# A scheduled recurrence and two gated layers on one core: GpSimd gets no tensor work, prices of the scheduler change, eight units keep separate states

## The chip, the cores and the metric

The kernel runs on one core of a Trainium2 chip. TensorE (PE, with its weight loads as PEld), VectorE (DVE), ScalarE (ACT), GpSimd (POOL) and SyncE (SP, which issues all DMAs) each work through a list of instructions of their own, and wait for each other by semaphores. The metric is the device time of one execution in microseconds (us).

## The reference, cut to what matters

```python
for t in range(S):                                   # S = 768, B = 2, H = 8, D = 48
    cur = einsum('bhd,bhe->bhde', u * k[t], v[t])
    y[t] = einsum('bhd,bhde->bhe', r[t], state + cur)
    state = w[t][..., None] * state + einsum('bhd,bhe->bhde', k[t], v[t])
x = y.reshape(B * S, 384)                            # 1536 tokens
xn = x / sqrt(mean(x * x) + 1e-6) * g
x = (silu(xn @ w_gate) * (xn @ w_val)) @ w_out       # 384 -> 1536 -> 384
x = ((x @ w_a) * (x @ w_b)) @ w_out2                 # the same sizes, without silu
```

Everything is float32. The kernel gets float32 products from TensorE in three passes of a rounded high part and a low part of each operand.

## The kernel before, in words

**The recurrence.** Time is cut into 12 units of 128 steps (6 for each of the two batches), and a unit into two halves of 64. `unit()` makes the scores of a half among themselves by levels of 1, 2, 4, 8, 16 and 32 steps: it multiplies the tile X (which holds r, k and the decays of the unit) by decays over growing distances (`upd`, L495 to L503, recorded at L460; T holds the decays, halved in width from level to level), stacks parts of it in RS and KS by small copies (L512 to L519, recorded at L293), multiplies these on TensorE (L524), and puts each level into its place in the score tile AA (fills at L484 and L487, picks at L545). TK holds k and r by tokens for the diagonal (L465 to L470).

Units with a number below `NSR` keep their state in tiles of their own, ST: the state is multiplied by the decay (into TMP, L614), the unit's own products are added (L625), and the output is the sum of two sets of matmuls (L640), one with the scores and one with the state. Such a unit takes one of the two AA tiles for both halves and does fills and picks over 128 partitions. From unit `NSR` on, `stacked()` puts the state under the values V and the weights of the state under the scores in AA, so that one set of matmuls does both (L421); each half has an AA tile, so that fills and picks go over 64 partitions and are twice as many, and four more copies (L389) and the decay (L398) stack the rows.

A unit's output is normalised (L661 to L702; the tiny steps on NS are L671 to L683) and split into high and low part XS.

**The layers.** Tokens are in four blocks of three units. For each layer m, block j and slice f of the 12 slices of the inner width, `front` makes 18 matmuls of 384 columns (L755), the activation (ACT L762), a product (DVE L764) and the split of it (HS, L766 and L767); `back` makes 9 more matmuls (L776). That is a step here: 27 matmuls, 96 steps in all, 48 for each layer. Weights come as 64-bit words in the ring WST of 7 tiles (72 loads); `convert` (L714 to L737) makes two float32 tiles of each by shifts and by an or (L721 to L732), a rounding copy and the subtraction L735. The 36 conversions of layer 0 run beside the first steps, those of layer 1 beside steps 36 to 53.

**The order.** Nothing is written in order by hand. Each task has a rank, its possible engines with a price in ns, and what it reads and writes. `Plan.walk` takes the tasks by rank and by when an engine would be free, puts each on the engine where it would end first, and keeps a clock for each engine; prices with a third entry 1 hold a common port, one at a time. `Plan.issue` does 13 walks with ranks from the walk before, and issues the shortest. In the opening, before the first matmul of a front, TensorE's planned gaps are filled with matmuls on a blank tile (L812, "filler"). So a price changes no work, but the order on all engines. `load` gives the price of a DMA, `vg`, `vgr` and `vgs` those of the two-input operations that may go to VectorE ("V") or GpSimd ("G").

Of the kernel before, what the change touches and what calls it, by code (L numbers as in the profile page):

```python
# [21 lines left out]
UT = 128  # L22
# [6 lines left out]
LEVELS = (2, 4, 8, 16)  # L29
EPS = 1e-6  # L30
OUT = (128, 3, B * S)
NSR = 5


BK, WALKS, FILL0, PACE = 0.15, 13, 900, 1.1
# [4 lines left out]
class Plan:  # L40
# [41 lines left out]
    def walk(self, rank):  # L82
# [35 lines left out]
        for _ in range(n):  # L118
# [34 lines left out]
            if e == "P":  # L153

                fill = fill and self.cols[i] < 2.3
                if fill and start > FILL0:
                    clock[e] = max(clock[e], FILL0)
                    while start - clock[e] >= 110 or credit(clock[e]) < 0:
                        clock[e] += stream(clock[e], 110, 256 / 110)
                        order.append((clock[e], e, None, None))  # L160
                    start = max(start, clock[e])

                if self.cols[i] > 2.3 and not long:
                    start += 87
                long = self.cols[i] > 2.3
                cost = stream(start, cost, self.cols[i])
            if take is not None:
# [72 lines left out]
def rwkv_moe_kernel(  # L240
# [7 lines left out]
    add = plan.add  # L248
# [14 lines left out]
    def v1(n):  # L263
        return (("V", 65 + 1.04 * n),)
# [3 lines left out]
        return (("V", 65 + 1.04 * n, 1),)  # L268

    def vg(n):  # L270
        return (("V", 65 + 1.04 * n, 1), ("G", 240 + 2.08 * n, 1))


    def vgr(n):
        return (("V", 65 + 1.04 * n, 1), ("G", 180 + 1.667 * n, 1))

    def vgs(n):
        return (("V", 65 + 1.04 * n, 1), ("G", 147 + 2.0 * n, 1))

    def act(n):  # L280
        return (("A", 95 + 0.83 * n),)
# [1 line left out]
    def va(n):  # L283
        return (("V", 65 + 0.52 * n, 1), ("A", 95 + 0.83 * n))
# [1 line left out]
    def pe(ns):  # L286
        return (("P", ns),)

    def load(nbytes):
        return (("Q", nbytes / 360.0),)  # L290

    def copy(E, out, in_):
        (E.copy if E is nc.scalar else E.tensor_copy)(out=out, in_=in_)  # L293
# [63 lines left out]
    def dup(fn, *args):  # L357
        return lambda E: fn(E, *args)


    def load_unit(rank, u):
        b, c = divmod(u, NU)
        s, sv = turn(u, X, 2), turn(u, VS, 2)
        add(rank, load(112 * 6144), lambda E: E.dma_start(
            out=X[s], in_=ax[b, c].rearrange("p a b t -> p a (b t)")), w=[("R", s), ("K", s), ("T", s, 1)])
        for par in two:
            rr = slice(64 * par, 64 * par + 64)
            add(rank, load(64 * 1536), dup(lambda E, par, rr: E.dma_start(
                out=VS[sv][par][rr].rearrange("p h d -> p (h d)"), in_=av[u, rr]), par, rr), w=[("v", sv, par)])

    def load_tokens(rank, u):
        b, c = divmod(u, NU)
        k = turn(u, TK, 1)
        add(rank, load(128 * 4608), lambda E: E.dma_start(
            out=TK[k], in_=atk[u]), w=[("tk", k, 0), ("tk", k, 1)])

    def stacked(at, f, u, r_, t64, t64key, yp):
# [7 lines left out]
        for par in two:  # L385
            if first and par == 0:
                continue
            for hf in two:
                add(at + 12 * f, va(256), dup(lambda E, par, hf: copy(  # L389
                    E, AA[par][place[par]].rearrange("p (a f) t -> p a f t", f=2)[:, :, hf],  # L390
                    r_[rows(hf)].rearrange("p (a par t) -> p a par t", par=2, t=64)[:, :, par]), par, hf),
                    r=[("R", s)], w=[("aa", par, 7 + hf)], lock=("aa", par))

        def decay(E):
            for par in two:
                for hf in two:
                    copy(E, PW[place[par], :, hf], t64[rows(hf), :, par])
        add(at + 12 * f, (("V", 280), ("A", 400)), decay, r=[t64key], w=[("pw",)])  # L398
        up = ("up", u)

        def update(E):
# [45 lines left out]
    def unit(rank, drank, u):  # L447
# [60 lines left out]
        def products(at, g):  # L508
# [3 lines left out]
            for hf in two:  # L512
                def stack(E, hf):
                    copy(E, RS[q][rows(hf), :, hf].rearrange("p e (i h) -> p e i h", h=h), rv[rows(hf), :, :, 1])
                add(at, va(256), dup(stack, hf), r=[("R", s)], w=[("rs", q, hf)])
            j = (4 * u + g) % len(KS)
            left = KS[j]
            add(at, va(256), lambda E: copy(E, halves(left.rearrange("p e t -> p (e t)"), h)[:, :, 0], halves(k_, h)[:, :, 0]),
# [13 lines left out]
        def pick(at, key, g, rr, a):  # L532
            h = LEVELS[g]

            def fn(E):
# [7 lines left out]
                d = bank(key)[rr, 0:256].rearrange("p (e i h) -> p e i h", e=8, h=h)  # L543
                m = masks[rr, 1 + g].rearrange("p (x i h) -> p x i h", x=1, h=h)
                E.copy_predicated(o, m.to_broadcast([rr.stop - rr.start, 8, 32 // h, h]), d)  # L545
            where = v1(256) + ((("A", 5.0 * (rr.stop - rr.start)),) if h == 16 else ())
            add(at, where, fn, r=[key, ("aa", a, 0), ("masks",)], w=[("aa", a, 2 + g)], give=key, lock=("aa", a))

        upd(at, 1)
# [17 lines left out]
        for par in two:  # L567
            a = par if ar else sa
            for hf in two:
                def fn(E, par, hf, a):  # L570
                    r1, r2 = slice(64 * par, 64 * par + 32), slice(64 * par + 32 * hf, 64 * par + 32 * hf + 32)
                    copy(E, AA[a][r1].rearrange("p (a f) t -> p a f t", f=2)[:, :, hf, 32:64],
                         bank(lx)[r2, 0:NPAIR * 32].rearrange("p (a t) -> p a t", a=NPAIR))
                add(at + 11 * f, (("A", 160), ("V", 200)), dup(fn, par, hf, a), r=[lx, ("aa", a, 0)],
                    w=[("aa", a, 9 + 2 * par + hf)], give=lx, lock=("aa", a))
        upd(at + 11 * f, 32)
        kp = ("kp", u)
# [67 lines left out]
                r=[("v", sv, par), ("st", i % 3), ("R", s), ("z",)] + [("aa", sa, i_) for i_ in range(13)], w=[yp], take=yp if par == 0 else None)  # L645
        sx, sy = u % len(XT), u % len(Y3)
        xt, y3, ns = XT[sx], Y3[sy], NS[sn]
        add(at + 15 * f, (("A", 150),), lambda E: copy(E, y3, bank(yp)[0:112, 3 * UT:4 * UT]), r=[yp], w=[("y3", sy)], give=yp)
        add(at + 15 * f, (("V", 470), ("A", 380)), lambda E: copy(
            E, xt[0:112], bank(yp)[0:112, 0:3 * UT].rearrange("p (a t) -> p a t", a=3)),  # L650
            r=[yp], w=[("xt", sx, i) for i in range(7)], give=yp)
# [278 lines left out]
```

## Time and profile before

| | |
|---|---|
| median of 3 runs | 642.37 us (641.42 to 643.42) |
| the profiled execution's own time | 642.38 us |
| its span in the trace | 640.6 us |
| granted TensorE clock, mean over the span | 0.964 of full speed |
| PE, DVE, ACT, POOL busy | 597.0, 434.6, 258.6, 141.9 us |
| first matmul of a front | at 81.07 us |

Busy times are sums over the whole span; the stages differ, and the rows below give them stage by stage. A gap in brackets behind a row is the time that the engine stood idle just before, with what released it. Mean times of one instruction include the time in which it waited inside the engine.

### The profile page before, as it was taken

What the parts mean: (1) busy time and instruction counts of PE and PEld (TensorE: products, weight loads), DVE (VectorE), ACT (ScalarE), POOL (GpSimd) and SP (SyncE); (2) the same over time, 40 slices, a digit from 0 to 9 for tenths busy, and PEclk for the clock granted to TensorE, in tenths of its full rate; (3) what the DMA queues carried; (4) which work ended last, traced back from release to release, by engine and by line L of the source; (5) the groups of instructions that cost most, each with busy time, mean ns of one, the idle gap of its engine ahead of it and who ended that gap; (6) DMA issues with size and microseconds to landing.
All of it is one profiled execution on the core that took longest, in us unless ns stands there. A gap on an engine that the chain in (4) does not pass through costs nothing.

```text
span 640.6 us, 12599 instructions
## 1 busy us (share of the span) xinstructions
PE 597.0 (93%) x4977; PEld 555.1 (87%) x4977; DVE 434.6 (68%) x946; ACT 258.6 (40%) x622; POOL 141.9 (22%) x156
## 2 busy tenths in 40 slices
PE   5899998595998998999999998999999999999997
PEld 4677777484987887899899898999999999999997
DVE  4778989999999999988737898972333333233332
ACT  2654568695877553424311556741011011101101
POOL 5236325346354552130000214100000000000000
PEclk8888999598899999999999999999999999999999
DMA  8934265442452221100001446600010001001001
GB/s 215 300 101 126 63 183 181 150 124 100 143 189 86 87 83 53 45 17 2 5 5 33 141 127 218 198 2 0 1 38 1 0 2 38 1 0 38 1 0 38
DMA packets 20363, 50.15 MB, mean 78 GB/s; under 512 B 3600, under 2 KB 8208, under 8 KB 20304
## 3 DMA queue, kind: packets, MB, share of 16 engines
q1 hardware_dynamic: 20304, 49.35, 25.4%
q8 instruction: 39, 0.64, 0.4%
q14 instruction: 20, 0.16, 0.1%
HBM read 46.38 MB, written 2.36 MB: 76 GB/s over the span
## 4 chain that ended last, share of the span: by engine, by line
PE 59%; DVE 19%; DMA 8%; ACT 6%; issue 5%; SPq 1%; POOL 1%; DVEq 0%; ACTq 0%; POOLq 0%
PE ps L755 34%; PE ps L776 17%; DMA WST<-wt 6%; DVE X L460 2%; DVE WST L730 2%; PE ps L640 2%; PE ps L812 2%; DVE AA L545 2%; DVE WST L732 2%; PE ps L524 2%; DMA X<-ax 1%; DVE W L735 1%; ACT WST L726 1%; DVE HS L767 1%; SPq L654 1%
## 5 line engine op out<-in xcount | busy, mean ns | idle before, releaser
L755 PE MATMUL ps<-XS,W 128*128 128x384 f32 x1728 | 344.5, 343 | 21.5 <-DVE W L735 6.8
L755 PEld LDWEIGHTS ps<-XS,W 128*128 128x128 f32 x1728 | 303.9, 191 | 30.2 <-ACT H L762 10.4
L776 PE MATMUL ps<-HS,W 128*128 128x384 f32 x864 | 176.2, 336 | 3.6 <-DVE HS L767 3.6
L776 PEld LDWEIGHTS ps<-HS,W 128*128 128x128 f32 x864 | 151.4, 188 | 4.6 <-DVE HS L767 3.9
L762 ACT ACTIVATE H<-ps 128x384 f32<-128x384 f32 x96 | 47.1, 490 | 223.7 <-PE ps L755 203.2
L764 DVE TENSOR_TENSOR H<-ps,H 128x384 f32<-128x384 f32 x96 | 53.3, 556 | 83.9 <-ACT H L762 81.5
L293 DVE CAST HS<-H 128x384 fp32r<-128x384 f32 x66 | 25.7, 389 | 71.6 <-PE ps L776 71.5
L767 DVE TENSOR_TENSOR HS<-H,HS 128x384 fp32r<-128x384 f32 x90 | 53.2, 591 | 3.2 <-ACT HS L293 1.0
L721 ACT ACTIVATE WST<-WST 128x384 f32<-128x384 f32 x72 | 40.4, 562 | 26.5 <-DMA WST<-wt 25.8
L735 POOL TENSOR_TENSOR W<-WST,W 128x384 fp32r<-128x384 f32 x20 | 28.7, 1436 | 93.6 <-ACT W L293 48.1
L524 PEld LDWEIGHTS ps<-RS,KS 112*64 112x64 f32 x768 | 28.7, 149 | 16.0 <-issue 6.7
L730 DVE SCALAR_TENSOR_TENSOR WST<-WST 128x384 uint32<-128x384 uint32 x72 | 41.3, 585 | 0.2
L732 DVE SCALAR_TENSOR_TENSOR WST<-WST 128x384 uint32<-128x384 uint32 x72 | 41.0, 581 | 0.2
L293 ACT COPY RS<-X 48x256 f32<-48x256 f32 x74 | 30.2, 408 | 26.4 <-DVE X L460 17.4
L524 PE MATMUL ps<-RS,KS 112*64 112x64 f32 x768 | 35.3, 240 | 5.5 <-ACT RS L293 5.4
L460 DVE TENSOR_TENSOR X<-X,T 112x512 f32<-112x512 f32 x47 | 35.3, 751 | 5.2 <-ACT KS L293 2.5
L812 PE MATMUL ps<-H 128*128 128x256 bf16 x257 | 37.8, 299 | 1.1 <-DVE H L811 1.1
L293 ACT CAST W<-WST 128x384 fp32r<-128x384 f32 x59 | 31.6, 546 | 16.3 <-DVE WST L732 13.3
L545 DVE COPY_PREDICATED AA<-masks,ps 64x256 f32<-64x256 int32 (+1 forms) x64 | 33.4, 522 | 5.3 <-PE ps L524 3.5
L726 ACT ACTIVATE WST<-WST 128x384 uint32<-128x384 uint32 x62 | 34.1, 552 | 0.0
L735 DVE TENSOR_TENSOR W<-WST,W 128x384 fp32r<-128x384 f32 x52 | 31.8, 618 | 1.4 <-ACT W L293 1.1
L812 PEld LDWEIGHTS <-H 128*128 128x128 bf16 x257 | 25.7, 107 | 6.8 <-DVE H L811 1.1
(87 smaller groups left out, 496.5 us busy)
## 6 DMA issues: line engine op xcount, KB each, us to landing
WST<-wt SPq DMA_DIRECT2D x72, 384.0 KB, 3.7
X<-ax SPq DMA_DIRECT2D x12, 672.0 KB, 5.2
TK<-atk SPq DMA_DIRECT2D x12, 576.0 KB, 4.0
V<-av SPq DMA_DIRECT2D x24, 96.0 KB, 4.0
out<-XT SPq DMA_DIRECT2D x12, 192.0 KB, 1.9
XT<-Y SPq DMA_DIRECT2D x72, 8.0 KB, 2.6
u<-au SPq DMA_DIRECT2D x1, 192.0 KB, 4.0
masks<-cms SPq DMA_DIRECT2D x1, 80.0 KB, 10.3
```

The source lines that it names most:

```text
L293: (E.copy if E is nc.scalar else E.tensor_copy)(out=out, in_=in_)
L460: E.tensor_tensor(out=o, in0=a, in1=b_, op=ALU.mult)
L524: E.matmul(out=bank(key)[o:o + 64, 64 * (e // 2):64 * (e // 2) + 64], lhsT=left[:, e], rhs=RS[q][:, e].rearrange("p f t -> p (f t)"), star ...
L730: add(rank, vp(384), lambda E: E.scalar_tensor_tensor(out=x, in0=e, scalar=3, in1=x, op0=ALU.logical_shift_left, op1=ALU.bitwise_or), r=[t ...
L732: add(rank, vp(384), lambda E: E.scalar_tensor_tensor(out=x, in0=e, scalar=0x80000000, in1=x, op0=ALU.bitwise_and, op1=ALU.bitwise_or), r= ...
L735: add(rank, vg(384), lambda E: E.tensor_tensor(out=lo, in0=x.bitcast(F32), in1=hi.bitcast(F32), op=ALU.subtract), r=[tx, ("w", f, i, 0)], ...
L755: E.matmul(out=t, lhsT=W[f][:, a, 3 * which + kk], rhs=XS[j][:, b_, kk], start=(i == 0 and kk == 0), stop=(i == 2 and kk == 2),)
L762: add(n - boost, (("A", 375),), lambda E: E.activation(out=h, in_=gv[0][:, 0:BLK], func=AF.Silu if m == 0 else AF.Copy), r=[("gv", 0)], w= ...
L764: add(n - boost, v1(BLK), lambda E: E.tensor_tensor(out=h, in0=gv[1][:, 0:BLK], in1=h, op=ALU.mult), r=[("gv", 1)], w=[("h", qh)], wait=89)
L767: add(n - boost, vg(BLK), lambda E: E.tensor_tensor(out=hs[:, 1], in0=h, in1=hs[:, 0].bitcast(F32), op=ALU.subtract), r=[("h", qh), ("hs", ...
L776: E.matmul(out=acc[d], lhsT=W[f][:, a, 6 + d], rhs=hs[:, b_], start=(f == 0 and i == 0), stop=(f == NF - 1 and i == 2),)
L812: plan.filler = lambda E: E.matmul(out=gv[1][:, 0:256], lhsT=blank[:, 0:128], rhs=blank, start=True, stop=True, skip_group_check=True)
```

## The change

The prices of `vg`, `vgr` and `vgs` lose their GpSimd entry, so that GpSimd keeps only the memsets of the opening. `NSR` goes from 5 to 8: units 5, 6 and 7 keep separate states as units 0 to 4 do. The other edits are prices: a switch of TensorE between the long matmuls of the layers and the small ones now costs 90 ns both ways (before: 87 ns, one way), loads are dearer where X and TK are read, and small copies, picks and the decay are dearer.

```diff
-NSR = 5
+NSR = 8
...
-                if self.cols[i] > 2.3 and not long:
-                    start += 87
+                if (self.cols[i] > 2.3) != long:
+                    start += 90
...
     def vg(n):
-        return (("V", 65 + 1.04 * n, 1), ("G", 240 + 2.08 * n, 1))
+        return (("V", 65 + 1.04 * n, 1),)
     def vgr(n):
-        return (("V", 65 + 1.04 * n, 1), ("G", 180 + 1.667 * n, 1))
+        return (("V", 65 + 1.04 * n, 1),)
     def vgs(n):
-        return (("V", 65 + 1.04 * n, 1), ("G", 147 + 2.0 * n, 1))
+        return (("V", 65 + 1.04 * n, 1),)
...
-    def load(nbytes):
-        return (("Q", nbytes / 360.0),)
+    def load(nbytes, rate=380.0):
+        return (("Q", nbytes / rate),)
...
-        add(rank, load(112 * 6144), lambda E: E.dma_start(
+        add(rank, load(112 * 6144, 200.0), lambda E: E.dma_start(
...
-        add(rank, load(128 * 4608), lambda E: E.dma_start(
+        add(rank, load(128 * 4608, 250.0), lambda E: E.dma_start(
...
-        add(at + 12 * f, (("V", 280), ("A", 400)), decay, r=[t64key], w=[("pw",)])
+        add(at + 12 * f, (("V", 400, 1), ("A", 760)), decay, r=[t64key], w=[("pw",)])
...
-                add(at, va(256), dup(stack, hf), r=[("R", s)], w=[("rs", q, hf)])
+                add(at, (("V", 260, 1), ("A", 400)), dup(stack, hf), r=[("R", s)], w=[("rs", q, hf)])
...
-            where = v1(256) + ((("A", 5.0 * (rr.stop - rr.start)),) if h == 16 else ())
+            where = (("V", 440 if rr.stop - rr.start == 64 else 335),) + ((("A", 8.3 * (rr.stop - rr.start)),) if h == 16 else ())
...
-                add(at + 11 * f, (("A", 160), ("V", 200)), dup(fn, par, hf, a), r=[lx, ("aa", a, 0)],
+                add(at + 11 * f, (("A", 265), ("V", 260)), dup(fn, par, hf, a), r=[lx, ("aa", a, 0)],
```

The order of the built program shows three places. The first is VectorE at the start of unit 0 (X_85 is unit 0's X, X_86 unit 1's; the rows are those behind the reduction into DG_94). Before, these stand there:

```order
L460 TENSOR_TENSOR T_88<-X_85 112x256
L293 COPY RS_75<-X_85 48x8x32
L484 TENSOR_TENSOR AA_79<-maskd,DG_94 128x512
L460 TENSOR_TENSOR X_85<-X_85,T_88 112x2x128x2
L487 COPY_PREDICATED AA_79<-masks,DG_94 128x256
L293 COPY KS_78<-X_85 112x64x4
```

With the change the same place on VectorE reads:

```order
L460 TENSOR_TENSOR X_85<-X_85 112x2x256
L460 TENSOR_TENSOR T_88<-X_85 112x256
L293 COPY KS_77<-X_85 112x128x2
L293 COPY RS_75<-X_85 48x8x32
L484 TENSOR_TENSOR AA_79<-maskd,DG_94 128x512
L460 TENSOR_TENSOR X_85<-X_85,T_88 112x2x128x2
L460 TENSOR_TENSOR T_89<-T_88 112x128
L293 COPY KS_78<-X_85 112x64x4
L293 COPY RS_76<-X_85 48x8x32
```

The first product on X_85 and the halvings of T, which were GpSimd's, now stand between VectorE's own, and two more small copies are VectorE's. Over the program 138 operations on tensors move from GpSimd to VectorE, and VectorE's list grows from 946 to 1068 instructions.

The second place is TensorE at the first matmul of a front (XS_105 and W_118 are block 0 and slice 0; ps_64 and ps_65 are the two halves of a front). Before:

```order
L524 MATMUL ps_62<-RS_76,KS_78 64x64 x8
L755 MATMUL ps_64<-XS_105,W_118 128x384 x6
L755 MATMUL ps_65<-XS_105,W_118 128x384 x3
L755 MATMUL ps_64<-XS_105,W_118 128x384 x3
L755 MATMUL ps_65<-XS_105,W_118 128x384 x3
L640 MATMUL ps_63<-AA_80,V_81 64x64
```

With the change:

```order
L812 MATMUL ps_65<-H_107 128x256
L524 MATMUL ps_62<-RS_76,KS_78 64x64 x8
L755 MATMUL ps_64<-XS_105,W_118 128x384 x3
L581 MATMUL ps_63<-ident,X_86 128x112 x4
L755 MATMUL ps_64<-XS_105,W_118 128x384 x3
L599 MATMUL ps_62<-V_83,KT 64x48
```

The transposes (L581) and products (L599) of unit 4 now stand between the matmuls of the first front, where before unit 3's output (L640) stood behind most of it. Ahead of the first front the list holds 302 fillers instead of 257.

The third place is VectorE's picks of unit 5, which is the first one that changes its kind. Before, each level is picked twice over 64 partitions, with AA_79 and AA_80 for the two halves:

```order
L460 TENSOR_TENSOR X_137<-X_137,T_90 112x2x32x8
L545 COPY_PREDICATED AA_80<-masks,ps_63 64x128x2
L621 TENSOR_TENSOR V_139<-TMP,ps_61 48x4x48 x2
L545 COPY_PREDICATED AA_79<-masks,ps_62 64x64x4
L545 COPY_PREDICATED AA_80<-masks,ps_62 64x64x4
```

With the change a level is picked once over 128 partitions, into AA_80 alone:

```order
L545 COPY_PREDICATED AA_80<-masks,ps_62 128x64x4
L767 TENSOR_TENSOR HS_109<-H_107,HS_109 128x384
L732 SCALAR_TENSOR_TENSOR WST_112<-WST_112 128x384
L735 TENSOR_TENSOR W_125<-WST_111,W_125 128x384
L487 COPY_PREDICATED AA_80<-masks,DG_95 128x256
L730 SCALAR_TENSOR_TENSOR WST_113<-WST_113 128x384
L545 COPY_PREDICATED AA_80<-masks,ps_63 128x128x2
L545 COPY_PREDICATED AA_80<-masks,ps_61 128x32x8
```

In VectorE's list as a whole the picks over 64 partitions go from 46 to 28, those over 128 from 18 to 25; on TensorE L640 goes from 152 matmuls to 240 and L599 from 80 to 120, L421 from 112 to 64 and L405 from 96 to 56.

## Rows read from the trace of the kernel before

**Rows 1.** The page, busy time, share and instructions of each engine.

```profile
PE 597.0 (93%) x4977; PEld 555.1 (87%) x4977; DVE 434.6 (68%) x946; ACT 258.6 (40%) x622; POOL 141.9 (22%) x156
```

**Rows 2.** Windows: stretch, length, busy time of each engine, granted clock, DMA share, GB/s.

```profile
0.00:81.00 81.00, 71.14 (x1005) 55.53 (x1005) 59.95 (x144) 36.27 (x94) 35.19 (x57) 0.87 0.58 159
81.00:118.00 37.00, 28.66 (x332) 23.47 (x327) 33.93 (x65) 27.80 (x65) 14.34 (x9) 0.94 0.67 193
118.00:174.00 56.00, 46.25 (x369) 40.58 (x370) 52.27 (x119) 41.23 (x99) 25.73 (x21) 0.83 0.36 123
174.00:279.00 105.00, 97.71 (x1013) 88.70 (x1012) 100.90 (x216) 56.65 (x152) 43.59 (x50) 1.00 0.28 86
...
426.00:640.00 214.00, 210.72 (x1216) 210.40 (x1214) 67.89 (x139) 28.29 (x58) 0.00 (x0) 1.00 0.03 12
```

**Rows 3.** Groups by form on POOL, whole span: busy us, mean ns, idle before.

```profile
L735 POOL TENSOR_TENSOR W<-WST,W 128x384 fp32r<-128x384 f32 x20 | 28.7, 1436 | 93.6 <-ACT W L293 48.1 <-PE ps L755 21.5 <-DVE W L293 16.5
...
L484 POOL TENSOR_TENSOR AA<-maskd,DG 64x512 f32<-64x512 f32 x2 | 13.8, 6902 | 8.7 <-DVE DG L468 8.7
```

**Rows 4.** Groups by form on DVE, whole span.

```profile
L767 DVE TENSOR_TENSOR HS<-H,HS 128x384 fp32r<-128x384 f32 x90 | 53.2, 591 | 3.2 <-ACT HS L293 1.0
...
L730 DVE SCALAR_TENSOR_TENSOR WST<-WST 128x384 uint32<-128x384 uint32 x72 | 41.3, 585 | 0.2
L732 DVE SCALAR_TENSOR_TENSOR WST<-WST 128x384 uint32<-128x384 uint32 x72 | 41.0, 581 | 0.2
...
L460 DVE TENSOR_TENSOR X<-X,T 112x512 f32<-112x512 f32 x47 | 35.3, 751 | 5.2 <-ACT KS L293 2.5 <-PE ps L561 2.3
...
L735 DVE TENSOR_TENSOR W<-WST,W 128x384 fp32r<-128x384 f32 x52 | 31.8, 618 | 1.4 <-ACT W L293 1.1 <-PE ps L755 0.2
...
L545 DVE COPY_PREDICATED AA<-masks,ps 64x256 f32<-64x256 int32 x46 | 24.2, 527 | 2.2 <-ACT AA L293 0.9 <-PE ps L524 0.5
...
L484 DVE TENSOR_TENSOR AA<-maskd,DG 64x512 f32<-64x512 f32 x12 | 11.1, 925 | 1.3 <-PE ps L421 1.2
...
L683 DVE SCALAR_TENSOR_TENSOR NS<-NS 128x1 f32<-128x1 f32 x36 | 9.8, 272 | 0.4
```

**Rows 5.** The same view from 300 to 346 us, where POOL is nearly idle.

```profile
L460 DVE TENSOR_TENSOR X<-X,T 112x512 f32<-112x512 f32 x3 | 2.1, 695 | 1.4 <-PE ps L561 1.4
...
L683 DVE SCALAR_TENSOR_TENSOR NS<-NS 128x1 f32<-128x1 f32 x9 | 1.4, 158 | 0.2
...
L484 DVE TENSOR_TENSOR AA<-maskd,DG 64x512 f32<-64x512 f32 x1 | 0.7, 689 | 0.6 <-PE ps L421 0.6
```

**Rows 6.** The same view from 440 to 620 us, where POOL does nothing.

```profile
L767 DVE TENSOR_TENSOR HS<-H,HS 128x384 fp32r<-128x384 f32 x39 | 21.8, 559 | 1.4
```

**Rows 7.** Timeline, 106 to 118 us: start, length, instruction [idle before].

```profile
107.30 6.38 POOL L484 TENSOR_TENSOR AA<-maskd,DG 64x512 f32<-64x512 f32 x1 [2.49 <-DVE DG L468]
...
110.35 1.02 DVE L730 SCALAR_TENSOR_TENSOR WST<-WST 128x384 uint32<-128x384 uint32 x2
...
112.81 1.28 DVE L735 TENSOR_TENSOR W<-WST,W 128x384 fp32r<-128x384 f32 x1
...
116.31 1.33 PE L755 MATMUL ps<-XS,W 128*128 128x384 f32 x3 [6.61 <-DVE W L735]
```

**Rows 8.** Waits of DVE, 0 to 92 us: total, times, longest.

```profile
DVE TK L460 <- DMA TK<-atk: 7.2, 2, 3.6
...
DVE AA L545 <- PE ps L524: 3.0, 3, 1.2
...
DVE RS L293 <- POOL X L460: 1.4, 1, 1.4
```

**Rows 9.** The page's groups: fillers on PE.

```profile
L812 PE MATMUL ps<-H 128*128 128x256 bf16 x257 | 37.8, 299 | 1.1 <-DVE H L811 1.1
```

**Rows 10.** Timeline of PE, 81 to 82 us: the first front.

```profile
81.07 1.33 PE L755 MATMUL ps<-XS,W 128*128 128x384 f32 x6
```

**Rows 11.** The chain that ended last, 30 to 60 us: start, length, what.

```profile
41.50 2.05 PE ps L640 x24
```

More of the change, by code (lines that the diff above doesn't have):

```diff
@@ L388, in stacked @@
             for hf in two:
-                add(at + 12 * f, va(256), dup(lambda E, par, hf: copy(
+                add(at + 12 * f, (("V", 260, 1), ("A", 410)), dup(lambda E, par, hf: copy(
                     E, AA[par][place[par]].rearrange("p (a f) t -> p a f t", f=2)[:, :, hf],
@@ L647, in unit @@
         xt, y3, ns = XT[sx], Y3[sy], NS[sn]
-        add(at + 15 * f, (("A", 150),), lambda E: copy(E, y3, bank(yp)[0:112, 3 * UT:4 * UT]), r=[yp], w=[("y3", sy)], give=yp)
+        add(at + 15 * f, (("A", 210),), lambda E: copy(E, y3, bank(yp)[0:112, 3 * UT:4 * UT]), r=[yp], w=[("y3", sy)], give=yp)
         add(at + 15 * f, (("V", 470), ("A", 380)), lambda E: copy(
```

## Prediction

> **What bounds the kernel now.** I read the page's busy line first [rows 1]. PE is busy for 93% of the span and looks like the bound throughout; the windows say otherwise [rows 2]. From 426 us on PE is busy 210.72 of 214 us and GpSimd does nothing: the end is PE's queue, and whatever is late at 426 us is late at the end. Between 81 and 279 us it is VectorE that is full: 33.93 of 37, 52.27 of 56 and 100.90 of 105 us, together 187.1 of 198 us (94%), while PE has 8.3, 9.8 and 7.3 us idle, together 25.4 us. Up to 81 us, where the first front starts [rows 10], VectorE has 21.05 us idle and PE's list is padded with fillers. So three things decide: how much VectorE has to do until about 279 us, how much of its idle time before 81 us goes, and whether PE gets more work than the 25.4 us cover. The groups by form and the quiet windows [rows 3 to 6] give the prices, the timeline and the waits [rows 7, 8] the places.
>
> **GpSimd's work moves to VectorE.** 138 operations move, with 141.9 us of GpSimd's busy time less its memsets. Two like operations of VectorE of 0.55 us each took 1.02 us back to back [rows 7], so the second costs 0.47 us, and I take 0.09 us off each duration. A two-input operation on 128x384 takes 559 ns where GpSimd is idle [rows 6], so 0.47; 47 of those that move have that size (20 of L735, 6 of L767, 2 of XS, 14 of TK, 5 of V): 47 x 0.47 = 22.1 us. X products are 17, at 695 - 90 ns [rows 5]: 10.3 us. The AA fills are 3 at 0.60: 1.8 us. The narrower ones have no row of their own; between a step on one column (158 - 90 = 70 ns, [rows 5]) and 470 ns for 384 columns I take a straight line, an estimate: 8 of 256 columns at 0.34, 10 of 128 at 0.20, 8 of 64 at 0.14, 24 below that at 0.09, 6 of TMP at 0.27, 15 of SQ at 0.20, together 12.6 us (if all cost the 70 ns of the smallest, 5; at 470 ns each, 33). Sum: 46.8 us.
>
> **What VectorE gets back.** The same forms are faster where GpSimd is quiet. Against rows 4: L767 591 against 559 ns, times 90: 2.9 us. L735 618 against 559, times 52: 3.1. L730 and L732 585 and 581 against the same 559 (their size is the same), times 72 each: 1.9 and 1.6. X products 751 against 695, times 47: 2.6. L484 925 against 689, times 12: 2.8. L683, on a single column, 272 against 158, times 36: 4.1. That is 19.0 us on 223.5 us of busy time, 8.5%. The other forms have 211 us; I take the same share on two thirds of them, since products that read PSUM may not meet GpSimd at all: 12 us. Back come 31 us (19 if the rest gives nothing, 37 if all of it does).
>
> In the trace this is a contention that both sides pay: GpSimd's fill of 64x512 took 6.38 us, and L735 beside its end 1.28 instead of 0.56 us [rows 7]; GpSimd's mean for that fill was 6902 ns, for L735 1436 ns [rows 3]. The Trainium skill (SBUF — State Buffer, section "SBUF: two separate sides") says that the port pair shared by GpSimd and VectorE is an exclusive lock, held for the whole instruction, and the loser fully blocks. The trace agrees that GpSimd blocks (6.38 us for the fill); it shows VectorE's operations running on beside it, so it doesn't show VectorE locked out for GpSimd's busy time. By that rule every us in which GpSimd holds the pair comes back to VectorE's two-input operations, and more would return than the means show.
>
> **Three units change their kind.** By the counts of the order, VectorE and GpSimd together: picks fall by 9 net, at about 0.52 us [rows 4]: -4.7 us. Fills L484 and L487 fall by 3 each at 0.69 [rows 5]: -4.1. Products and sums on V fall by 8 at 0.55, those on TMP and ST rise by 8 at about 0.35 (half the columns): -1.6. Copies: 13 fewer of AA and PW, 16 more of RS, KS and W on VectorE, all about 0.3: +0.9. Sum -9.5 us (the copies at nothing or twice as many: -10 to -8).
>
> So VectorE has 46.8 - 31 - 9.5 = +6 us to do (0 to +18 by the bounds of the contention), nearly all before 279 us, where nothing covers it.
>
> On PE L640 rises by 88 matmuls at 2.05 / 24 = 0.085 us [rows 11], and 40 more of L599 stand against 48 of L421 and 40 of L405 that go. These have no row here; at the same 0.085 they give -4.1 us, so the sum is +3.4, and +7.5 if they were free. It lies between 118 and 240 us, where PE has idle time; I cost it at nothing. If the cover is gone, 4 us.
>
> **Idle time of VectorE in the opening.** Up to 92 us it waits 1.4 us for GpSimd's X product, and twice 3.6 us for TK [rows 8]; the first of the two is the load at the start and stays, the second is unit 2's, and in the new order more of unit 0's and 1's work (GpSimd's before) stands ahead of it, so that the load has landed. Of the 3.0 us in which it waits for L524, half can be filled by what is moved. Together -6.5 us (0, if the longer serial list opens gaps of its own, to -12).
>
> The first front will not start earlier for this: VectorE has more to do before it, and PE has 45 more fillers at 37.8 / 257 = 0.147 us [rows 9], 6.6 us, beside more of unit 4. I expect it at 86 to 92 us instead of 81.07. The work that is done before is missing later: unit 4's transposes stand in the first front now.
>
> **The stretch from 81 us on.** PE lost 6.61 us in one gap, waiting for a conversion's L735 [rows 7], while GpSimd sat on the fill that the plan had priced at 180 + 1.667 x 512 = 1034 ns. The order was made for a chip on which that fill takes 1 us. With no operation priced so wrongly, VectorE's list should wait less at such places; I take two thirds of this gap, -4.5 us (0 to -6.6). The prices of copies, loads and switches move things I can't name one by one; I cost them at nothing, with 3 us to either side: the conversions' stretch behind 350 us has the same work as before.
>
> **Sum.** +6 - 6.5 - 4.5 + 0 = -5 us against the profiled execution's 642.38 us (span 640.6 us and 1.8 us around it), which is the median of the runs to within 0.01 us: 637 us. Range of this case alone: 631 to 640.
>
> **The rivals.** *VectorE gains less than it takes over.* If the contention returns only the 19 us that rows 4 to 6 show, VectorE has 46.8 - 19 - 9.5 = +18 us to do; the 6.5 us of idle time go with it and the gap at 116 us does not shrink, since VectorE is later, not earlier: +11.5, or 654 us; halfway to the forecast's contention 648 us. It decides from the point where the return falls below 46.8 - 9.5 - 6.5 - 4.5 = 26 us. For it speaks that VectorE is 94% busy from 81 to 279 us and now the only engine for this work; against it, that L683's loss of 114 ns on a single column shows a contention the big forms hide.
>
> *The lock gives back more.* GpSimd is busy 83.7 us between 81 and 279 us [rows 2]. If VectorE's operations stand still for more of this than their mean times show, and 45 us instead of 31 come back, VectorE falls by 8 us instead of rising by 6. PE can then regain at most its idle 25.4 us, less 4 us of new work; with half of that, 10.5 us, and 1.5 more for the opening, 630 us. (This is the direction in which the lock of the Trainium skill's page on SBUF would take it.) Against it: beside the fill of 6.38 us VectorE's rows run on at 0.55 us.
>
> *Nothing is left over.* The 6 us more and the idle time less cancel: 641 to 644 us. For it speaks that both terms are small against their bounds.
>
> **How the numbers follow.** Forecast (637) 0.34, the lock (630) 0.13, nothing left 0.19, VectorE the loser (648) 0.34. Within 0.3% (1.9 us) is about what a measurement of this kernel can't tell from no change. A small part of the forecast (down to 640.4) counts as faster, so faster 0.47, same 0.19, slower 0.34. The range 628 to 650 leaves out the far ends of the first rival and of the lock.
>
> **What would show it.** The first L755 at 86 to 92 us; VectorE's busy time between 81 and 279 us still 93% or more of the stretch; L683 near 160 ns and L484 near 690 ns all over the span; L767 near 559. The stretch behind 426 us unchanged in its rate. The forecast is wrong if VectorE's busy time up to the last unit has grown by more than 10 us, if PE's gaps behind L735 are as large as before, or if PE shows less than 10 us idle between 81 and 279 us and is itself the bound there.

## The result, and the profile after

| | before | after |
|---|---|---|
| median on the same chip | 642.37 us (641.42 to 643.42) | 624.03 us (620.85 to 624.5) |
| span of the profile shown | 640.6 us | 623.5 us |
| ratio | | 0.97 [0.9645, 0.9755] |

The forecast was 637 us with a range of 628 to 650; the change brought 18.3 us, over three times the 5 us forecast. One slow execution of each kernel (660.92 us before; 722.55 us after, at a granted clock of 0.746) is left out here, as such ones are of every ratio below, and since the recorded profile is of the latter, every row of after here is from a second set of runs of the same program (e1 below), whose profiled execution took 625.35 us.

The page's busy line after:

```profile
PE 599.8 (96%) x5102; PEld 557.8 (89%) x5102; DVE 432.3 (69%) x1068; ACT 251.3 (40%) x607; POOL 4.8 (1%) x18
```

Beside [rows 1]: GpSimd has gone from 141.9 us to its memsets, VectorE does 122 instructions more (1068 against 946), and yet it is busy 2.3 us less. The windows of after (columns as in [rows 2]):

```profile
0.00:81.00 81.00, 76.57 (x1115) 59.39 (x1116) 63.52 (x183) 36.59 (x98) 4.77 (x18) 0.94 0.61 171
81.00:118.00 37.00, 31.03 (x279) 25.88 (x277) 35.33 (x92) 28.31 (x67) 0.00 (x0) 0.97 0.56 175
118.00:174.00 56.00, 52.26 (x532) 46.46 (x532) 55.45 (x141) 46.04 (x114) 0.00 (x0) 0.93 0.47 146
174.00:279.00 105.00, 100.43 (x1074) 91.88 (x1071) 101.72 (x255) 51.29 (x139) 0.00 (x0) 1.00 0.24 71
...
426.00:620.00 194.00, 193.67 (x1118) 193.35 (x1116) 61.49 (x125) 25.46 (x53) 0.00 (x0) 1.00 0.03 10
```

Between 81 and 279 us VectorE is fuller still (192.5 of 198 us, before 187.1), the granted clock is higher (0.93 against 0.83 from 118 to 174 us), and behind 426 us PE is full as before. Fixed times mix the stages of two kernels, though. So both are cut where the same work of the layers is done: at the first matmul of step 24 (the 649th long matmul: 24 x 27 = 648). In before:

```profile
0.00:278.80 278.80, 243.56 (x2709) 208.08 (x2710) 246.85 (x539) 161.95 (x408) 118.84 (x135) 0.92 0.44 129
...
278.80:640.60 361.80, 353.43 (x2270) 346.98 (x2268) 187.71 (x407) 96.62 (x214) 23.01 (x21) 1.00 0.12 39
```

and after:

```profile
0.00:263.30 263.30, 245.96 (x2834) 210.83 (x2835) 241.00 (x633) 154.87 (x394) 4.77 (x18) 0.96 0.46 136
...
263.30:623.50 360.20, 353.84 (x2270) 346.92 (x2268) 191.33 (x436) 96.44 (x213) 0.00 (x0) 1.00 0.13 40
```

The time up to step 24 is VectorE's busy time and its idle time: 246.9 + 31.9 before, 241.0 + 22.3 after. So of the 17.1 us between the spans 5.9 are less work of VectorE, 9.6 less idle time of it, and 1.6 lie behind step 24. This is a sum and not yet a cause; the experiments ask what the parts of it do. The forms of VectorE after (shape and count; busy us, mean ns; idle before):

```profile
L767 DVE TENSOR_TENSOR HS<-H,HS 128x384 fp32r<-128x384 f32 x96 | 53.4, 556 | 1.9
...
L460 DVE TENSOR_TENSOR X<-X,T 112x512 f32<-112x512 f32 x60 | 41.3, 689 | 1.8 <-PE ps L561 1.4 <-ACT RS L293 0.2
L732 DVE SCALAR_TENSOR_TENSOR WST<-WST 128x384 uint32<-128x384 uint32 x72 | 39.2, 552 | 0.2
L735 DVE TENSOR_TENSOR W<-WST,W 128x384 fp32r<-128x384 f32 x72 | 39.2, 551 | 1.0 <-ACT W L293 0.5 <-PE ps L755 0.2
...
L683 DVE SCALAR_TENSOR_TENSOR NS<-NS 128x1 f32<-128x1 f32 x36 | 5.6, 156 | 0.3
...
L484 DVE TENSOR_TENSOR AA<-maskd,DG 64x512 f32<-64x512 f32 x8 | 5.5, 684 | 0.2
```

Against [rows 4] each is back at its price in the quiet stretch [rows 5, 6]: from 591 to 556 ns for L767, and from 272 to 156 ns for the single column of L683. Waits of DVE, 0 to 92 us (total, times, longest), and two places of PE's timeline:

```profile
DVE RS L293 <- PE ps L524: 4.5, 2, 4.3
DVE AA L545 <- PE ps L524: 3.7, 2, 2.6
DVE TK L460 <- DMA TK<-atk: 3.4, 1, 3.4
```

```profile
85.21 0.76 PE L755 MATMUL ps<-XS,W 128*128 128x384 f32 x3 [1.11 <-DVE W L293]
...
115.40 0.79 PE L755 MATMUL ps<-XS,W 128*128 128x384 f32 x3 [1.55 <-DVE W L735]
```

Beside [rows 8] the wait for POOL and the second wait for TK are gone, but those for L524 grew from 3.0 to 8.2 us. The first front starts at 85.21 us instead of 81.07 [rows 10], and the gap behind L735 near 115 us is 1.55 us instead of 6.61 [rows 7].

### The profile page after: what moved, and what is told of

The parts are those of the page before. It is cut to its first block, busy times and chain, and to the rows that moved or that the text cites. A ratio compares the mean times of both kernels' runs of the same rounds, so it can differ in the third digit from the quotient of the medians.

```text
span 720.8 us, 12726 instructions
## 1 busy us (share of the span) xinstructions
PE 708.9 (98%) x5102; PEld 624.5 (87%) x5102; DVE 437.2 (61%) x1068; ACT 253.2 (35%) x607; POOL 4.8 (1%) x18
## 4 chain that ended last, share of the span: by engine, by line
PE 94%; DVE 4%; DMA 1%; issue 0%; SPq 0%; ACT 0%; ACTq 0%; DVEq 0%
PE ps L755 51%; PE ps L776 25%; PE ps L812 5%; PE ps L524 4%; PE ps L640 4%; PE ps L599 1%; DMA X<-ax 1%; PE ps L581 1%; PE ps L421 1%; PE ps L561 1%; DVE X L460 1%; PE ps L405 1%; DVE WST L732 1%; PE ps L685 0%; DVE W L735 0%
## 5 line engine op out<-in xcount | busy, mean ns | idle before, releaser
L755 PE MATMUL ps<-XS,W 128*128 128x384 f32 x1728 | 405.3, 390 | 2.3 <-DVE W L735 1.5
L755 PEld LDWEIGHTS ps<-XS,W 128*128 128x128 f32 x1728 | 337.3, 201 | 31.5 <-DVE W L735 1.6
L776 PE MATMUL ps<-HS,W 128*128 128x384 f32 x864 | 211.7, 388 | 1.6 <-DVE HS L767 1.6
L776 PEld LDWEIGHTS ps<-HS,W 128*128 128x128 f32 x864 | 169.5, 201 | 16.2 <-DVE HS L767 2.0
L767 DVE TENSOR_TENSOR HS<-H,HS 128x384 fp32r<-128x384 f32 x96 | 53.5, 557 | 6.3 <-ACT HS L293 4.0
L812 PE MATMUL ps<-H 128*128 128x256 bf16 x302 | 50.1, 323 | 1.1 <-DVE H L811 1.1
L460 DVE TENSOR_TENSOR X<-X,T 112x512 f32<-112x512 f32 x60 | 41.3, 688 | 4.9 <-PE ps L561 4.6
L293 ACT COPY RS<-X 48x256 f32<-48x256 f32 x69 | 28.2, 408 | 39.7 <-DVE X L460 24.8
L524 PEld LDWEIGHTS ps<-RS,KS 112*64 112x64 f32 x768 | 30.6, 159 | 12.7 <-issue 9.4
L812 PEld LDWEIGHTS <-H 128*128 128x128 bf16 x302 | 31.7, 112 | 10.8 <-DVE H L811 1.1
L735 DVE TENSOR_TENSOR W<-WST,W 128x384 fp32r<-128x384 f32 x72 | 39.3, 552 | 1.1 <-ACT W L293 0.5
L730 DVE SCALAR_TENSOR_TENSOR WST<-WST 128x384 uint32<-128x384 uint32 x72 | 39.2, 553 | 0.0
L524 PE MATMUL ps<-RS,KS 112*64 112x64 f32 x768 | 36.9, 251 | 1.6 <-DVE NS L680 1.1
L545 DVE COPY_PREDICATED AA<-masks,ps 64x256 f32<-64x256 int32 (+1 forms) x53 | 27.5, 519 | 7.7 <-PE ps L524 6.3
L293 ACT COPY AA<-ps 32x128 f32<-32x128 f32 (+1 forms) x84 | 21.6, 257 | 16.1 <-PE ps L524 5.7
```

Of the source, the lines that this page charges most:

```text
L460: E.tensor_tensor(out=o, in0=a, in1=b_, op=ALU.mult)
L524: E.matmul(out=bank(key)[o:o + 64, 64 * (e // 2):64 * (e // 2) + 64], lhsT=left[:, e], rhs=RS[q][:, e].rearrange("p f t -> p (f t)"), star ...
L735: add(rank, vg(384), lambda E: E.tensor_tensor(out=lo, in0=x.bitcast(F32), in1=hi.bitcast(F32), op=ALU.subtract), r=[tx, ("w", f, i, 0)], ...
L755: E.matmul(out=t, lhsT=W[f][:, a, 3 * which + kk], rhs=XS[j][:, b_, kk], start=(i == 0 and kk == 0), stop=(i == 2 and kk == 2),)
L767: add(n - boost, vg(BLK), lambda E: E.tensor_tensor(out=hs[:, 1], in0=h, in1=hs[:, 0].bitcast(F32), op=ALU.subtract), r=[("h", qh), ("hs", ...
L776: E.matmul(out=acc[d], lhsT=W[f][:, a, 6 + d], rhs=hs[:, b_], start=(f == 0 and i == 0), stop=(f == NF - 1 and i == 2),)
```

## The experiments

All sixteen kernels are read by the same sum: time to step 24 (VectorE's busy + idle), then the time behind it. The second part is 355 to 363 us in all of them. There is one profile of each. Times are medians; ratios are against runs of the kernel before on the same chip, with 95% intervals, and aren't always the quotients of the medians beside them.

### The change run again (e1), and GpSimd's work on VectorE in the old order (e2)

> The changed kernel as it is, for an undisturbed profile. Every theory expects the time already seen, 621 to 625 us. Theory 1 (VectorE: it loses nothing to GpSimd any more) expects VectorE's busy time between 81 and 279 us at or below the 187.1 us of before, L683 near 160 ns, L484 near 690 ns, and the layers' steps ahead of the old kernel's from 118 us on. Theory 2 (clock: TensorE is busier and keeps its full clock) expects the granted clock of the stretch 81 to 174 us, 0.94 and 0.83 before, at 0.97 or more, and VectorE no less loaded than before.

621.11 us (620.25 to 625.35), ratio 0.98 [0.9734, 0.9865]; the kernel before took 636.2 us on that chip, and its 19 runs lay between 629.65 and 642.44. Neither theory had all its signs: VectorE's busy time between 81 and 279 us rose to 192.5 us (Theory 1 had it at or below 187.1, while L683 at 156 ns and L484 at 684 came as it said), and the granted clock was 0.97 and 0.93 from 81 to 118 and from 118 to 174 us (Theory 2 had 0.97 or more in both).

In e2 the walk still counts on GpSimd, but its operations are issued on VectorE at the places where GpSimd had them:

```diff
-                self.tasks[i][2](self.engines[e])
+                self.tasks[i][2](self.engines["V" if e == "G" and len(self.cost[i]) > 1 else e])
```

> The kernel before with its old plan, but every operation that the plan gave to GpSimd is issued on VectorE at the same place of the order (138 operations; the memsets stay). Work and order of everything else are the same. Theory 1 (contention): what comes back is as much as what is added, so 632 to 643 us although the plan thinks two engines work; L683 near 160 ns. Theory 2 (the order, made with true prices, is what matters): VectorE's list is longer in an order that doesn't know it, 643 to 655 us.

641.72 us (640.25 to 645.49), ratio 1.012 [1.0054, 1.0186]. Windows to step 24 and behind it:

```profile
0.00:279.90 279.90, 239.60 (x2709) 202.90 (x2710) 258.82 (x654) 162.21 (x407) 4.76 (x18) 0.95 0.43 128
...
279.90:640.40 360.50, 353.57 (x2269) 346.93 (x2268) 188.60 (x431) 96.81 (x216) 0.00 (x0) 1.00 0.12 40
```

Taken over in all: 258.82 + 188.60 = 447.4 us, 12.8 more than before. The prediction had 46.8 - 31 = 15.8. So taking the work off GpSimd and changing nothing else costs VectorE 13 us, and the kernel wins nothing by it: by the ratio it is 1.2% slower. The profile is 1.1 us later at step 24, since VectorE has 12.0 us more to do there and 10.9 us less idle time (31.9 became 21.1), in the old order.

### The parts alone and in pairs (e3 to e8)

Each is a part of the change, made in the kernel before. G (e3, with N in e8, with P in e6) takes the GpSimd entry from `vg`, `vgr` and `vgs`:

```diff
     def vgr(n):
-        return (("V", 65 + 1.04 * n, 1), ("G", 180 + 1.667 * n, 1))
+        return (("V", 65 + 1.04 * n, 1),)
```

N (e5, with P in e7) keeps eight states apart:

```diff
-NSR = 5
+NSR = 8
```

P (e4) is all other prices of the change, as in:

```diff
-                if self.cols[i] > 2.3 and not long:
-                    start += 87
+                if (self.cols[i] > 2.3) != long:
+                    start += 90
...
-        add(at + 12 * f, (("V", 280), ("A", 400)), decay, r=[t64key], w=[("pw",)])
+        add(at + 12 * f, (("V", 400, 1), ("A", 760)), decay, r=[t64key], w=[("pw",)])
```

> The kernel before with only the GpSimd entries of the three price functions taken away; prices and five separate states as before. Theory 1 expects most of the gain here: 625 to 632 us. Theory 2 expects half or less, 632 to 642 us, since the prices of copies and loads are still wrong.

> The kernel before with only the new prices (switches, loads, small copies, picks); GpSimd keeps its entries and five units keep separate states. Theory 1 expects little: 637 to 645 us. Theory 2 expects at least half of the gain, 626 to 634 us, and a granted clock of 0.98.

> The kernel before with only NSR 8 instead of 5: units 5 to 7 keep separate states; GpSimd and the old prices stay. So far: prices alone gave -6.5 us, no GpSimd alone -1.2, the whole change -15. Theory A (the parts add up, and the states are worth the rest): 627 to 630 us. Theory B (the parts need each other: only a plan with all true prices uses the freed VectorE time): 634 to 642 us, no change.

> The changed kernel with NSR back at 5: no GpSimd work and new prices, five separate states. Theory A (the states are worth 7 us): 626 to 630 us. Theory B: 620 to 624 us, as fast as the whole change.

> The changed kernel with GpSimd's entries back: new prices, eight separate states. Theory A (GpSimd alone is worth 1 us): 621 to 625 us. Theory B: 628 to 633 us, as slow as the prices alone.

> The changed kernel with the old prices of switches, loads, copies and picks: no GpSimd work, eight separate states. Theory A: 626 to 630 us (the prices' 6.5 us are missing). Theory B: 632 to 638 us, since without the prices the rest is worth nothing, as in the run without GpSimd.

e3 and e4 came as Theory 2 had it, e6 as Theory A, e7 as Theory B; e5 fell between its two theories, and e8 came out faster than both.

| parts | run | median | ratio | to step 24: DVE busy + idle | DVE busy in all |
|---|---|---|---|---|---|
| none | before | 636.2, 637.82 on these chips | 1 | 246.9 + 31.9 | 434.6 |
| G | e3 | 634.99 | 0.9972 [0.9932, 1.0012] | 247.2 + 25.1 | 442.5 |
| P | e4 | 629.75 | 0.9948 [0.9925, 0.9972] | 248.1 + 24.6 | 430.3 |
| N | e5 | 630.93 | 0.9894 [0.9815, 0.9974] | 235.9 + 38.7 | 425.0 |
| G, P | e6 | 628.46 | 0.9865 [0.9811, 0.9919] | 247.9 + 18.5 | 444.5 |
| P, N | e7 | 632.83 | 0.9925 [0.9895, 0.9955] | 243.2 + 30.1 | 430.5 |
| G, N | e8 | 625.22 | 0.9816 [0.9755, 0.9877] | 237.1 + 24.2 | 427.3 |
| G, P, N | e1 | 621.11 | 0.98 [0.9734, 0.9865] | 241.0 + 22.3 | 432.3 |

The rows to step 24 of e4, e6 and e7, in this order:

```profile
0.00:272.70 272.70, 244.50 (x2768) 209.87 (x2769) 248.06 (x531) 161.24 (x404) 140.02 (x153) 0.95 0.43 132
0.00:266.40 266.40, 241.95 (x2735) 205.73 (x2735) 247.87 (x637) 160.81 (x408) 4.77 (x18) 0.96 0.44 135
0.00:273.30 273.30, 247.21 (x2851) 212.34 (x2852) 243.17 (x540) 151.86 (x379) 103.78 (x134) 0.96 0.44 132
```

Those of e5 and of e8, the widest pair (eight states with GpSimd, and without):

```profile
0.00:274.60 274.60, 246.65 (x2771) 211.61 (x2772) 235.95 (x530) 153.30 (x380) 109.68 (x129) 0.93 0.42 131
```

```profile
0.00:261.30 261.30, 239.42 (x2753) 203.80 (x2754) 237.11 (x620) 161.07 (x410) 4.76 (x18) 0.97 0.44 137
```

GpSimd's 109.68 us are gone, VectorE issues 90 instructions more and is busy 1.2 us more; its idle time falls by 14.5. In all four pairs the removal of G lowers the idle time (31.9 to 25.1, 24.6 to 18.5, 38.7 to 24.2, 30.1 to 22.3), and the busy time to step 24 moves by -2.2 to +1.2 us. The parts don't seem to add: by the ratios G alone brings 0.3%, which can't be told from zero, 0.8% beside N (e5 to e8) or beside P (e4 to e6), and 1.25%, 8 us, beside both (e7 to e1). N alone brings 1.1%, but beside P, with GpSimd at work, it makes the kernel 3 us slower (e4 to e7).

Not much can be built on one such step. Each row is one order, and the last experiments show orders of one kernel that lie 19 us apart. The profile of before is of an execution 6 us above its median on this chip, so most of the first pair's 6.8 us of idle time isn't in the medians (636.2 and 634.99 us). And e6 is 6.3 us ahead of e4 at step 24, but 5.8 us longer behind it (355.1 and 360.9 us). What all four pairs agree on is the sign of the idle time.

And e3 against e2 shows what the walk does with the knowledge that GpSimd is out:

```profile
0.00:272.30 272.30, 241.06 (x2684) 204.32 (x2685) 247.24 (x625) 167.86 (x427) 4.76 (x18) 0.94 0.45 132
...
272.30:635.00 362.70, 353.97 (x2270) 346.73 (x2268) 195.22 (x446) 95.84 (x213) 0.00 (x0) 1.00 0.13 39
```

Up to step 24 VectorE has 247.24 us instead of e2's 258.82. ScalarE has 4.7 us more in all (263.7 against 259.0) and VectorE 5.0 us less (copies of AA and RS for the most part); VectorE's work behind step 24, where PE is the limit and VectorE has room, grew from 188.6 to 195.2 us.

### Is VectorE's work the price? GpSimd busy beside it (e9), its work doubled (e10)

In e9 the order of all engines is that of after, and GpSimd gets 216 products of 128x128 that nobody needs, on weights that a conversion has just made (they add work, and leave none out):

```diff
+            if m == 0:
+                for k in range(6):
+                    nc.gpsimd.tensor_tensor(
+                        out=scratch, in0=hi[:, k % 3].bitcast(F32), in1=lo[:, k % 3].bitcast(F32), op=ALU.mult)
```

> The changed kernel with its order unchanged on VectorE, TensorE, ScalarE and SyncE; beside each of layer 0's 36 conversions GpSimd multiplies six pieces of 128x128 of the converted weights into a scratch tile that nobody reads (216 operations, some 100 us of GpSimd between about 70 and 175 us). Nothing waits for them. Theory 1 (VectorE loses time to a working GpSimd): GpSimd's 137 us of tensor work cost VectorE about 34 us before, a quarter, so VectorE gets about 20 to 30 us more to do in that stretch, and the end comes 12 to 25 us later: 633 to 646. Theory 2 (GpSimd beside costs little; the order made the gain): 621 to 626.

655.14 us (650.87 to 660.56), ratio 1.0316 [1.0237, 1.0396]. Its windows, and from its groups by form the added operation and two of VectorE (L737 and L684 are L735 and L683 above):

```profile
0.00:295.70 295.70, 259.07 (x2835) 218.20 (x2836) 275.12 (x633) 156.53 (x394) 174.16 (x234) 0.92 0.42 122
...
295.70:656.50 360.80, 354.28 (x2269) 346.62 (x2267) 191.51 (x436) 96.37 (x213) 0.00 (x0) 1.00 0.13 39
```

```profile
L740 POOL TENSOR_TENSOR scratch<-W 128x128 f32<-128x128 f32 x216 | 169.4, 784 | 93.7 <-DVE W L737 76.9
...
L737 DVE TENSOR_TENSOR W<-WST,W 128x384 fp32r<-128x384 f32 x72 | 42.2, 592 | 1.5 <-ACT W L293 1.3
...
L684 DVE SCALAR_TENSOR_TENSOR NS<-NS 128x1 f32<-128x1 f32 x36 | 7.9, 221 | 0.3
```

The same 633 instructions of VectorE to step 24 are busy 275.1 us instead of 241.0, +34.1; the span grows by 33.0. So 169.4 us of GpSimd beside VectorE cost VectorE 34 us, a fifth, and in this order VectorE's time before step 24 is the kernel's, one to one. The median lies above Theory 1's 633 to 646 us, with 169 us of GpSimd instead of some 100.

This also answers the clock. TensorE's list is that of after and nothing was added to it, yet its granted clock to step 24 fell from 0.96 to 0.92, as low as before, and VectorE's idle time didn't grow (20.6 us, 22.3 in e1). So here the lower clock comes with VectorE's lateness and isn't what makes VectorE wait; and e2, at 0.95, gained nothing.

The Trainium skill (SBUF — State Buffer, section "SBUF: two separate sides") has the loser fully blocked for a GpSimd operation that reads SBUF beside a VectorE operation with two SBUF inputs; the runs show a loss of a fifth of GpSimd's busy time over the mix of VectorE's operations here, so what of it is full blocking stays open. A block for a whole instruction is not what [rows 7] show: beside GpSimd's fill of 6.38 us (both inputs in SBUF) VectorE's L730, with two SBUF inputs as well, ran on at about 0.5 us each.

e10 keeps after's order and does fills L484, L487 and VectorE's picks of units 5 to 7 twice (15 operations more):

```diff
+                for _ in range(2 if 5 <= u < 8 else 1):
+                    E.copy_predicated(o, m.to_broadcast([rr.stop - rr.start, 8, 32 // h, h]), d)
```

> The changed kernel with its order unchanged, where the fills (L484, L487) and VectorE's picks (L545) of units 5, 6 and 7 are done twice, the second time with the same result: some 17 more operations of VectorE, about 9 us by rows of before, roughly what the three separate states save. Theory 1 (VectorE's work before 279 us is priced one to one): 628 to 632. Theory 2 (the states help by letting units overlap in the two score tiles, and VectorE's work is covered): 621 to 625.

636.28 us (632.52 to 639.21), ratio 1.0009 [0.9976, 1.0041].

```profile
0.00:272.40 272.40, 247.97 (x2834) 212.79 (x2835) 250.07 (x648) 154.96 (x394) 4.76 (x18) 0.96 0.45 132
...
272.40:633.60 361.20, 354.35 (x2270) 346.82 (x2268) 191.45 (x436) 96.30 (x213) 0.00 (x0) 1.00 0.13 39
```

9.1 us more work of VectorE, 10.1 us more span of the profiles. By the ratios e10 is 2.1% (13 us) behind e1, above the 628 to 632 us of Theory 1; so the price is at least one to one, and where more than that came from isn't shown.

### Is it the change, or the luck of one order? (e11 to e16)

Each walk is greedy, so a price that is off by 1 ns makes another order. The price of `vp` is 65 + 1.04 n in both kernels. Here it is 66 in after (e11) and in before (e12); e15 and e13 have 64, e16 and e14 have 67 in the same line:

```diff
-        return (("V", 65 + 1.04 * n, 1),)
+        return (("V", 66 + 1.04 * n, 1),)
```

> The changed kernel with one price moved by 1 ns (66 instead of 65 in the price of VectorE's conversions): the same work in another order, hundreds of rows different. It shows what an order alone is worth. Theory 1 (the amounts of work decide): within 4 us of the changed kernel, 618 to 626. Theory 3 (the plan's luck decides): anywhere from 615 to 640.

> The kernel before with the same price moved by 1 ns: the same kind of plan, with GpSimd, the old prices and five separate states, in another order. Theory 1: within 4 us of the kernel before, 632 to 642. Theory 3: it may come out as fast as the changed kernel, 615 to 632, or far slower.

> The kernel before with the price of VectorE's conversions at 64 instead of 65 ns: another order, the same work. So far the old kernel in two orders gave 636 and 650 us. If GpSimd at work is what makes VectorE stand idle before step 24 (25 to 41 us in the five kernels that use GpSimd), 630 to 655 us, idle 25 to 45 us. If the old order was only unlucky, 615 to 630.

> The same with 67 ns. The same expectations: 630 to 655 with an idle of 25 to 45 us if GpSimd makes it; 615 to 630 if it was luck.

> The changed kernel with that price at 64 ns. If the amounts of work decide, 618 to 627 us with VectorE busy some 241 us before step 24 and idle 18 to 25. If the order's luck decides, it scatters as the old kernel does, 615 to 640.

> The same with 67 ns. The same expectations: 618 to 627 with an idle of 18 to 25 us, or a scatter of 615 to 640.

| price | before: median, ratio | DVE busy + idle to step 24 | after: median, ratio | DVE busy + idle to step 24 |
|---|---|---|---|---|
| 64 | e13 652.67, 1.0184 [0.9967, 1.0401] | 258.1 + 28.2 | e15 620.73, 0.9685 [0.9525, 0.9845] | 242.4 + 15.2 |
| 65 | 635 to 642 | 246.9 + 31.9 | 621.11 and 624.03 | 241.0 + 22.3 |
| 66 | e12 649.95, 1.0206 [1.0142, 1.0269] | 251.3 + 40.6 | e11 621.74, 0.9799 [0.9748, 0.9851] | 240.9 + 20.2 |
| 67 | e14 634.12, 0.9894 [0.9737, 1.0051] | 243.8 + 30.1 | e16 619.53, 0.9667 [0.9475, 0.9858] | 238.3 + 15.0 |

e13 to e16 have two executions each.

Up to step 24, the other orders of the old kernel (e12, e13, e14) and of the changed one (e11, e15, e16):

```profile
0.00:291.90 291.90, 253.46 (x2718) 218.34 (x2719) 251.25 (x527) 161.04 (x407) 120.60 (x145) 0.90 0.40 123
0.00:286.30 286.30, 240.61 (x2710) 206.22 (x2711) 258.13 (x542) 161.00 (x405) 112.22 (x137) 0.94 0.40 125
0.00:273.90 273.90, 239.78 (x2717) 204.69 (x2718) 243.84 (x530) 165.49 (x419) 120.23 (x140) 0.94 0.43 131
```

```profile
0.00:261.10 261.10, 248.77 (x2896) 215.25 (x2897) 240.91 (x630) 156.82 (x397) 4.76 (x18) 0.99 0.46 138
0.00:257.60 257.60, 240.01 (x2820) 205.25 (x2821) 242.43 (x633) 155.64 (x390) 4.76 (x18) 0.99 0.45 139
0.00:253.30 253.30, 241.21 (x2814) 207.16 (x2815) 238.28 (x628) 157.00 (x395) 4.76 (x18) 0.99 0.47 142
```

The old kernel's four orders lie between 634 and 653 us, the changed one's between 619.5 and 624. They don't overlap: the gain is the change's, 10 to 15 us against the best old order, about 30 against the worst. VectorE's time splits as cleanly: the changed orders have less busy time (238.3 to 242.4 against 243.8 to 258.1 us) and less idle time (15.0 to 22.3 against 28.2 to 40.6). On the mean of four orders each these are 9.4 us less to do and 14.5 us less idle. Both scatter in the old kernel, busy time by 14 us and idle time by 12; in the changed one by 4 and 7. Of the expectations, e12 fell outside Theory 1's 632 to 642 us, and e15 and e16 have less idle time than the 18 to 25 us expected; the other times lie in a stated range.

## Why the prediction was right and wrong

The frame held: PE's queue is the end, VectorE fills the stretch before it, and in the order of after what VectorE does there costs the kernel at least one to one (e9, e10); in the old order 10.9 of e2's 12.0 us more went into idle time. The contention was sized well. The failed step is the sum that closed the work: VectorE "+6 us to do ..., nearly all before 279 us, where nothing covers it". Before step 24 it had 5.9 us less to do, 12 us beside the forecast, and this isn't one order's luck: over the four orders each it is 9.4 us less on the mean, and no changed order has as much to do as any old one. The path e2, e3, e8, e1 goes from before to after one part at a time (each edge is one order against another, so by the nudged orders an edge of a few us may be luck; the ends are not):

| edge | forecast | DVE busy in all | to step 24 | idle to step 24 |
|---|---|---|---|---|
| before to e2: work moved, contention back | +15.8 | +12.8 | +12.0 | -10.9 |
| e2 to e3: the walk knows that GpSimd is out | 0 | -5.0 | -11.6 | +4.0 |
| e3 to e8: eight states | -9.5 | -15.1 | -10.1 | -0.9 |
| e8 to e1: the other prices | 0 | +5.0 | +3.9 | -1.9 |
| sum | +6 | -2.3 | -5.9 | -9.6 |

- *Work moved less what comes back*: 12.8 for 15.8. If the 46.8 us moved are right, 34 us came back, not 31; the two weren't measured apart. The rival in which VectorE loses (19 back, 648 us) falls.
- *The new order at nothing*: this is the largest part of the miss, -11.6 us to step 24, or -7.7 with the other prices' +3.9 (on a path through e6 instead of e8 the prices give +0.6). The prediction took each operation that leaves GpSimd as one for VectorE, at once, before step 24. The walk of e3, which sees a full VectorE, gave copies to ScalarE (4.7 us) and let 6.6 us of work wait until behind step 24, where VectorE has some 170 us to spare. In the changed kernel the relief by ScalarE is gone again (251.3 us in all, 257.2 in e8, 258.6 before): the new prices make its copies of RS dearer, and VectorE does 27 of them instead of e8's 17. What stays is 3.6 us more work of VectorE behind step 24 than before (191.3 against 187.7).
- *Eight states*: -9.5 by count. In all it is -9.6 and +0.2 with GpSimd at work (e5, e4 to e7), -12.2 and -15.1 without it (e6 to e1, e3 to e8), on the mean -9.2; to step 24 it is -10.9, -4.9, -6.9 and -10.1. The size was right on the mean, and that the path above hits it is luck.
- *Idle time of the opening*: up to the first front 21.05 us became 17.6, -3.5 for -6.5. The two waits named went (5.2 us up to 92 us), but those for L524 grew by as much; the net gain comes from smaller waits.
- *The gap behind L735 and the like*: 6.61 became 1.55 us, -5.1 for -4.5, but the reading behind it is wrong. It has VectorE's list wait in that gap, while the window of the gap in before has VectorE busy for 6.53 of its 6.61 us (third pair of numbers); PE waited for a full VectorE, which the first term counts already:

```profile
109.70:116.31 6.61, 0.00 (x1) 0.00 (x1) 6.53 (x12) 5.21 (x12) 5.43 (x3) 0.78 0.86 269
```

  What did fall is VectorE's idle time between first front and step 24, elsewhere, from 10.9 to 4.7 us. The two idle terms together were forecast at -11 us: -9.6 in this pair of orders, -14.5 on the mean of four. That the first is so near is in part luck.
- *PE's extra work at nothing*: right. PE still has 14.3 us idle between 81 and 279 us (25.4 before), so it isn't the bound there. That it is busy 2.8 us more in all, for 3.4, says little: 45 more fillers are in it.
- *The stretch behind*: right, -1.6 us.
- *The other signs*: L683 156 for 160, L484 684 to 686 for 690, L767 556 for 559. The first front came at 85.21 us, just ahead of 86 to 92.

"The lock gives back more" was nearest in time (630 us), but not for its reason: VectorE got back about 34 us, not 45. "Nothing is left over" falls.

Left open: which of the price edits matter (they weren't split); why eight states with GpSimd leave 38.7 us of idle time (e5); and through what the idle time falls when GpSimd goes. Only 1.4 us of waits name POOL in the opening, yet 6 to 15 us go. A new order isn't needed for it: e2 keeps the old one and has 21.1 us, as the moved work stands where VectorE stood idle. But e2 has 12 us more work for it, and the change has less of both. One reading of that is that the old walk plans 1034 ns for a fill that takes 6.9 us [rows 3], and so orders VectorE's list for a time that doesn't come; the scatter of the orders (19 us with GpSimd, under 5 with the change) fits that. Against it, VectorE didn't stand idle beside the one fill looked at above. No run had GpSimd at right prices, so it isn't shown.

## What to carry to other kernels

Where a planner places the work, a moved operation isn't added to the engine that it falls to: ask which other engine, and which later stretch with slack, takes what overflows. A second engine isn't free either: here GpSimd cost VectorE a fifth of its own busy time (e9). That its short prices spoiled the order too, and that leaving it out is worth more with other changes than alone, is likely here and not shown. And before a gain of a few per cent is put down to a change, run each kernel in three or four slightly different orders.

## What was not expected of the hardware

- GpSimd's two-input work came back as VectorE's busy time at about a fifth of its length: 34 us for 169.4 us in e9. The single-column L683 suffers most in proportion: 272 ns before, 221 in e9, 156 with GpSimd quiet, while a 128x384 product rose from 551 to 592 in e9. It isn't only the shortest, nor only operations with two inputs: VectorE's copies into KS, with one input, took 489 ns before, 307 in e9 and 285 after (the rows of before and after):

```profile
L293 DVE COPY KS<-X 112x256 f32<-112x256 f32 x15 | 7.3, 489 | 0.2
L293 DVE COPY KS<-X 112x256 f32<-112x256 f32 x18 | 5.1, 285 | 0.3 <-PE ps L524 0.2
```

- The kernel before spread over 629.65 to 642.44 us in 19 runs of one order on one chip, 12.8 us and so nearly as much as the change is worth there (15.1 us by the medians); the changed kernel's four runs beside it spread over 5 us.
